# Four quarter-width column tiles for a GLU gate, and w_down's rows in the same order: one decode step on one Trainium2 core

## The chip, the core and the metric

The kernel runs on one core of a Trainium2 chip. The core has a matrix engine (TensorE, PE in the profile), a vector engine (DVE), an activation engine (ACT), GpSimd (POOL) and a sync engine (SP). Here SP and ACT issue all transfers. Sixteen DMA engines carry them from the chip's memory into the SBUF, the on-chip memory of 128 partitions. Matrix products go into PSUM. The metric is the device time of one execution in microseconds; the time before is the median of three runs.

## The reference

A decode step for one token: `x` has 512 values. It is normalized, and goes into an attention over 32 heads with 8192 cached keys and values of 128 elements each, and beside it into a gated unit whose result scales that of the attention.

```python
xn = _layernorm(x, axis=-1)                        # 512 values
# attention: wq [512, 4096], caches [1, 32, 8192, 128], wo [4096, 512]
q = (xn @ wq).reshape(B, Sq, H, Dh).transpose(0, 2, 1, 3)
scores = einsum("bhqd,bhkd->bhqk", q, k_cache) * (Dh ** -0.5)
o = einsum("bhqk,bhkd->bhqd", softmax(scores), v_cache)
s = o.transpose(0, 2, 1, 3).reshape(B, Sq, H * Dh) @ wo
# gated unit: w_gate and w_up [512, 1376], w_down [1376, 512]
h = sigmoid(xn @ w_gate) * (xn @ w_up)
g = silu(h @ w_down)
out = x + s * g
```

All of it is float32. The two caches hold 134 MB each (32 x 8192 x 128 x 4 bytes), wq and wo 8.4 MB each, the three matrices of the gated unit 2.8 MB each.

## The kernel before

The kernel treats two heads as a pair. A pair's keys are 16384 rows of 128 values; each partition takes 128 of them, 64 KB in a row. Three buffers of that size, `slots[0]` to `slots[2]`, hold what is in flight: the keys of pair `i` go to `slots[i % 2]`, all values to `slots[2]`. For each pair DVE multiplies the keys by the query (L276) and sums (L277), PE and ACT turn the scores into powers, and PE multiplies these with the values (L250). The normalized result of a pair is put into `o_all` by two small transfers that ACT issues (`place`, L298), of four rows each.

All large transfers go through SP's queue in the order in which they are written, each behind the waits that free its buffer. `load` (L121) issues one transfer and gives it a semaphore; the transfer is done when the semaphore has gone up by 16.

At the end of the loop the queue holds, in this order: the last pair's values into `slots[0]` (L326), `w_gate` and `w_up` (L330 and L331) into `slots[2]` once the matmuls of the values before are done, `w_down` in two transfers behind them (L332 and L333), and `wo` in six pieces into `slots[1]` (L336 to L338), once DVE is done with the last keys. `wo`'s partition `p` holds rows 32p to 32p + 31; `W_ENDS` cuts these 32 rows into pieces of 14, 10, 4, 2, 1 and 1.

The gate (L341 to L387) comes behind the loop on every engine. PE works with one vector of the normalized `x` as its stationary operand, so a matmul has a single output row; four such rows, at the partitions 0, 32, 64 and 96 of a PSUM bank, are called column tiles here (`NG = 4`, `GP = 32`). With F = 1376 the sizes are `FP = 10`, `FW = 320`, `FL = 96` and `FH = 352`. For each of `w_gate` and `w_up`, and each of the `KT = 4` parts of the contraction, tile `g` multiplies columns 320g to 320g + 319 in one matmul, which covers the first 1280 columns. The 96 columns that remain are done by three of the four tiles in matmuls of 32 columns (the loop over `g1` to `NG`). Tile 0 has nothing there, so DVE first zeroes its 32 places in the bank of the up-projection (L343), and PE waits for that.

ACT takes the sigmoid (L355), DVE multiplies (L358) and turns the row of each tile into columns by ten transposes of 32x32 blocks and one more for the last 32 places (L360 to L362). After that, `hid[p, c]` is hidden value 10p + c. So `w_down` is loaded with rows 10p to 10p + 9 in partition `p` (L332), and its last 128 rows, one in each partition, into `wd_last` (L333). PE multiplies the eleven columns (L377), the four partial rows are copied by ACT and folded by PE (L364 to L374), and ACT and DVE form the silu (L385 and L387).

Then PE goes through `wo` (L390 to L409), piece by piece as the pieces land. DVE multiplies by the gate, adds `x`, and SP stores the output (L411 to L416).

Of the kernel before, what the change touches and what calls it, by code (L numbers as in the profile page):

```python
# [13 lines left out]
P = 128  # L14
# [4 lines left out]
def kernel(  # L19
# [14 lines left out]
    D = x.shape[-1]  # L34
    F = w_gate.shape[1]
    KT = D // P
# [3 lines left out]
    NG = 4  # L40
    GP = P // NG
    GC = D // NG
    QT = 512
    HT = QT // Dh
    NQ = H * Dh // QT
# [3 lines left out]
    SLOT = NB * Dh  # L49
    HALF = (slice(0, HP), slice(HP, P))  # L50

    FP = F // P
    FL = F - FP * P
    FW = FP * GP
    FH = FW + GP
    assert FH <= QT and FL % GP == 0 and 2 * KT * F + FP * D <= SLOT

    W_ENDS, W_FOLD = (14, 24, 28, 30, 31, 32), 28

    PE, DVE, ACT, SP, POOL = nc.tensor, nc.vector, nc.scalar, nc.sync, nc.gpsimd  # L60
# [3 lines left out]
    def sb(name, *shape):  # L64
        return nc.alloc_sbuf_tensor(name, [P, *shape], F32)[:]

    def bank(name, rows, cols):
        return nc.alloc_psum_tensor(name, [rows, cols], F32)[:]


    x_col, xc, sq, xn = (sb(n, KT) for n in ("x_col", "xc", "sq", "xn"))
# [12 lines left out]
    wd_last = q_all[:, :D]  # L84
    sg, hg, s_tmp = (q_all[:, a:a + n] for a, n in ((D, FH), (D + FH, FH), (D + 2 * FH, QT)))
    assert D + 2 * FH + QT <= NP * Dh and FH <= QT

# [3 lines left out]
    o1 = sb("o1", QT)  # L91
    hid = o1[:, :(FP + 1) * GP].rearrange("p (c i) -> p c i", i=GP)

    o_all = sb("o_all", WR)

    big = [bank(f"big{i}", P, QT) for i in range(2)]
# [7 lines left out]
    def semaphore(name):  # L104
        sems.append(nc.alloc_semaphore(name))
        return sems[-1]
# [11 lines left out]
    pe, dve, act, pool = (Steps(n) for n in ("s_pe", "s_dve", "s_act", "s_pool"))  # L118
    loads = {}

    def load(eng, name, dst, src, *after):  # L121
        wait(eng, *after)
        if name not in loads:
            loads[name] = [semaphore(f"s_{name}"), 0]
        loads[name][1] += 16
        eng.dma_start(dst, src).then_inc(loads[name][0], 16)  # L126
        return loads[name][0], loads[name][1]

    def wait(eng, *steps):
        for s in steps:  # L130
            if s is not None:
                eng.wait_ge(*s)
# [42 lines left out]
    t = dve(DVE.reduce_sum(st[:, 0:1], x_col, axis=AX.X))  # L175
    wait(PE, t)
    t = pe(PE.matmul(pt[:, 0:1], ones, st[:, 0:1], start=True, stop=True))
    wait(DVE, t)
    t = dve(DVE.tensor_scalar(st[:, 1:2], pt[:, 0:1], 1.0 / D, None, op0=ALU.mult))
    wait(DVE, t)  # L180
    t = dve(DVE.tensor_scalar(xc, x_col, st[:, 1:2], None, op0=ALU.subtract))
    wait(DVE, t)
    t = dve(DVE.tensor_mul(sq, xc, xc))
    wait(DVE, t)
    t = dve(DVE.reduce_sum(st[:, 2:3], sq, axis=AX.X))
    wait(PE, t)
    t = pe(PE.matmul(pm[:, 0:1], ones, st[:, 2:3], start=True, stop=True))
    wait(ACT, t, c_eps)
    t = act(ACT.activation(st[:, 3:4], pm[:, 0:1], AF.Sqrt, bias=eps_t, scale=1.0 / D))
    wait(DVE, t)  # L190
    t = dve(DVE.reciprocal(st[:, 4:5], st[:, 3:4]))
# [5 lines left out]
    for k in range(KT):  # L197
        for b in range(NQ // NG):
            for g in range(NG):
                c = (b * NG + g) * QT  # L200
                ins = PE.matmul(big[b][g * GP:g * GP + 1, :], xn[:, k:k + 1], wq_t[:, k, c:c + QT],  # L201
                                start=(k == 0), stop=(k == KT - 1))
# [6 lines left out]
    spreads, copies = {}, {}  # L209
    for t in range(NQ):  # L210
        b, g = divmod(t, NG)
        wait(PE, c_row if t == 0 else None, copies.get(t - 2))
        spreads[t] = pe(PE.matmul(big[t % 2], ones[g * GP:g * GP + 1, :], q_row[g * GP:g * GP + 1, b, :],  # L213
                                  start=True, stop=True))

        for u in (t,) if t < NQ - 2 else (NQ - 2, NQ - 1) if t == NQ - 1 else ():
            wait(ACT, spreads[t])
            q = big[u % 2].rearrange("p (i e d) -> p i e d", e=2, d=Dh)
# [108 lines left out]
    t = slots[2]  # L327
    wg_t, wu_t = (t[:, n * KT * F:(n + 1) * KT * F].rearrange("p (k f) -> p k f", f=F) for n in range(2))
    wd_t = t[:, 2 * KT * F:2 * KT * F + FP * D].rearrange("p (c e) -> p c e", e=D)
    ld_g = load(SP, "wg", wg_t, w_gate.rearrange("(p k) f -> p k f", k=KT), (valued, NP - 1))  # L330
    ld_u = load(SP, "wu", wu_t, w_up.rearrange("(p k) f -> p k f", k=KT))  # L331
    load(SP, "wd", wd_t, w_down[:FP * P, :].rearrange("(p r) e -> p r e", r=FP))  # L332
    ld_d = load(SP, "wd", wd_last, w_down[F - P:, :])  # L333
    wo_t = slots[(NP - 1) % 2].rearrange("p (r e) -> p r e", e=D)
    ld_o = []
    for n, (r0, r1) in enumerate(zip((0,) + W_ENDS, W_ENDS)):  # L336
# [1 line left out]
                         summed[NP - 1] if n == 0 else None))  # L338


    g0 = (P - FL) // GP  # L341
    wait(DVE, copies[NQ - 1])
    c_zero = dve(DVE.memset(big[1][:g0 * GP, FW:FH], 0.0))  # L343
    wait(PE, c_zero)
    rows = []
    for dst, src, ld in ((big[0], wg_t, ld_g), (big[1], wu_t, ld_u)):
        wait(PE, ld)
        for c0, f0, w, g1 in ((0, 0, FW, 0), (FW, F - P, GP, g0)):
            for k in range(KT):
                for g in range(g1, NG):  # L350
                    ins = PE.matmul(dst[g * GP:g * GP + 1, c0:c0 + w], xn[:, k:k + 1],
                                    src[:, k, f0 + g * w:f0 + (g + 1) * w], start=(k == 0), stop=(k == KT - 1))
        rows.append(pe(ins))
    wait(ACT, rows[0])
    t = act(ACT.activation(sg, big[0][:, :FH], AF.Sigmoid))  # L355
    wait(DVE, t, rows[1])
    c_p4 = dve(DVE.memset(big[0], 0.0))
    t = dve(DVE.tensor_mul(hg, sg, big[1][:, :FH]))  # L358
    wait(DVE, t)
    for c in range(FP):  # L360
        dve(DVE.transpose(hid[:, c, :], hg[:, c:FW:FP]))
    t = dve(DVE.transpose(hid[:, FP, :], hg[:, FW:]))  # L362

    def to_fold(after):  # L364
        wait(ACT, after)
        return act(ACT.copy(s_tmp, big[0]))
# [10 lines left out]
    for c in range(FP + 1):  # L377
        g = c % NG * GP
        ins = PE.matmul(big[0][g:g + 1, :], hid[:, c, 0:1], wd_t[:, c, :] if c < FP else wd_last,
                        start=(c < NG), stop=(c + NG > FP))  # L380
    t = to_fold(pe(ins))
# [3 lines left out]
    t = act(ACT.activation(g_row, big[1][:, :GC], AF.Sigmoid))  # L385
# [6 lines left out]
    for ld, r1 in zip(ld_o, W_ENDS):  # L392
        wait(PE, ld)
        for r in range(r0, r1):
            if r < W_FOLD:
                g = r % NG * GP
                ins = PE.matmul(big[0][g:g + 1, :], o_all[:, r:r + 1], wo_t[:, r, :],  # L397
                                start=(r < NG), stop=(r + NG >= W_FOLD))
                continue
            for g in range(NG):  # L400
                ins = PE.matmul(acc[g * GP:g * GP + 1, :], o_all[:, r:r + 1], wo_t[:, r, g * GC:(g + 1) * GC],  # L401
                                start=(r == W_FOLD), stop=(r == WR - 1))
# [8 lines left out]
    t = dve(DVE.tensor_mul(g_row, g_row, acc))  # L411
    wait(DVE, t)
    t = dve(DVE.tensor_add(g_row, g_row, x_row))  # L413
# [37 lines left out]
```

## Time and profile before

| what | value |
|---|---|
| median of 3 runs | 687.94 us (687.91 to 688.11) |
| the profiled execution | 687.58 us |
| its span, first to last instruction | 685.8 us |
| mean granted TensorE clock | 0.659 |
| DVE busy | 574.0 us, 84% of the span |
| PE busy | 226.5 us, 33% |
| read from the chip's memory | 293.74 MB, 428 GB/s over the span |

The profile is a page on one execution, and a trace behind it that answers questions. Times in it are microseconds from the start of the span unless marked ns. An engine is busy while an instruction runs on it; "idle before, releaser" names the engine or the transfer that let the next instruction go. The profiled execution took 687.58 us, 1.78 us more than its span, and 0.36 us less than the median of the runs.

### The profile page before, as it was taken

Reading aid. Unit: us, or ns where it says so; the run is one execution under the profiler, and the core shown is the slowest. Engines: PE = TensorE matmul, PEld = TensorE weight load, DVE = VectorE, ACT = ScalarE, POOL = GpSimd, SP = SyncE. Lnnn points to the kernel's source line nnn. Section 1 sums busy time; section 2 is a strip of 40 time slices with the busy share of each in tenths; the row PEclk is TensorE's granted clock in tenths of the full one; section 3 lists DMA queues with packets and bytes.
Section 4 is the critical chain, followed back from the end, with each engine's and each line's share of the span. In section 5 each row is a group of like instructions: output and inputs, shape, how many; then the busy total and the mean of one; then the engine's idle time right before and its main releaser. Section 6 shows DMA issues by size and latency. Waiting matters only on the chain.

```text
span 685.8 us, 3690 instructions
## 1 busy us (share of the span) xinstructions
PE 226.5 (33%) x1570; PEld 63.8 (9%) x1570; DVE 574.0 (84%) x136; ACT 40.9 (6%) x122; POOL 0.7 (0%) x6
## 2 busy tenths in 40 slices
PE   0650230506042240605042150605042150506666
PEld 0110000101000010101000010101001010101121
DVE  1059999999999999989898989989898989989220
ACT  0030100000000000000001010000001010000010
POOL 0000000000000000000000000000000000000000
PEclk9955575756657575757566575757557575756898
DMA  8999999999999999999999999999999999999996
GB/s 371 459 441 436 432 428 428 428 432 428 428 432 466 433 436 428 432 428 432 428 428 428 443 459 432 432 428 432 432 428 428 428 443 451 440 432 428 406 431 283
DMA packets 6614, 293.84 MB, mean 428 GB/s; under 512 B 1096, under 2 KB 1104, under 8 KB 1616
## 3 DMA queue, kind: packets, MB, share of 16 engines
q1 hardware_dynamic: 6200, 293.74, 99.0%
q10 hardware_dynamic: 408, 0.02, 0.0%
q8 instruction: 4, 0.07, 0.0%
q14 instruction: 2, 0.02, 0.0%
HBM read 293.74 MB, written 0.00 MB: 428 GB/s over the span
## 4 chain that ended last, share of the span: by engine, by line
DMA 36%; DVE 30%; SPq 1%; PE 0%; issue 0%
DMA slot<-in_A_k_cache_dram 31%; DVE slot L276 15%; DVE sc L277 15%; DMA slot<-in_A_wo_dram 5%; SPq L126 1%; PE pt L241 0%; PE acc L401 0%; DVE g_row L411 0%; DVE g_row L413 0%; DVE mx L271 0%
## 5 line engine op out<-in xcount | busy, mean ns | idle before, releaser
L276 DVE TENSOR_TENSOR slot<-slot,q_all 128x16384 f32<-128x16384 f32 x16 | 275.5, 17217 | 48.3 <-DMA slot<-in_A_k_cache_dram 48.3
L277 DVE TENSOR_REDUCE sc<-slot 128x128 f32<-128x16384 f32 x16 | 275.5, 17220 | 0.6
L250 PE MATMUL po<-slot,weights 128*8 128x512 f32 x1024 | 148.0, 743 | 231.5 <-PEq L237 230.8
L250 PEld LDWEIGHTS po<-slot,weights 128*8 128x8 f32 x1024 | 30.3, 104 | 336.0 <-issue 335.2
L241 PE MATMUL pt<-ident,mx 128*1 128x128 f32 x32 | 8.7, 372 | 148.6 <-PEq L237 148.6
L296 ACT COPY o<-po 128x512 f32<-128x512 f32 x16 | 9.4, 585 | 385.9 <-PE po L250 385.9
L255 PE MATMUL pn<-o,pick 128*2 128x128 f32 x128 | 16.5, 272 | 12.8 <-PEq L237 12.8
L241 PEld LDWEIGHTS pt<-ident,mx 128*1 128x1 f32 x32 | 1.8, 80 | 154.1 <-issue 154.1
L289 ACT ACTIVATE nb<-pm 128x2 f32<-128x2 f32 x16 | 2.8, 172 | 190.3 <-PE pm L243 190.3
L283 DVE RECIPROCAL rl<-pn 2x1 f32<-2x1 f32 x16 | 2.3, 146 | 13.8 <-PE pn L255 13.8
L291 ACT ACTIVATE weights<-sc,nb 64x128 f32<-64x128 f32 x32 | 12.8, 399 | 0.9
L255 PEld LDWEIGHTS pn<-o,pick 128*2 128x2 f32 x128 | 9.9, 84 | 29.6 <-issue 27.2
L201 PE MATMUL big<-slot,xn 128*1 128x512 f32 x64 | 9.6, 768 | 7.5 <-DMA slot<-in_A_wq_dram 7.5
L411 DVE TENSOR_TENSOR g_row<-g_row,acc 128x128 f32<-128x128 f32 x1 | 0.3, 286 | 13.6 <-PE acc L401 13.6
L243 PE MATMUL pm<-mx,ones 1*128 1x2 f32 x32 | 8.8, 343 | 7.4 <-PEq L237 7.4
L245 PE MATMUL pn<-rs,half 128*2 128x1 f32 x32 | 3.0, 163 | 23.6 <-PEq L237 23.6
L397 PE MATMUL big<-slot,o_all 128*1 128x512 f32 x56 | 9.6, 802 | 2.9 <-DMA slot<-in_A_wo_dram 2.9
L213 PE MATMUL big<-q_all,ones 1*128 1x512 f32 x16 | 9.7, 1011 | 1.7 <-ACT q_all L220 0.8
L175 DVE TENSOR_REDUCE st<-x_col 128x1 f32<-128x4 f32 x1 | 0.2, 157 | 10.9 <-DMA x_col<-in_A_x_dram 10.9
L243 PEld LDWEIGHTS pm<-mx,ones 1*128 1x128 f32 x32 | 7.9, 306 | 14.3 <-issue 14.3
L271 DVE TENSOR_REDUCE mx<-pt 1x2 f32<-1x128 f32 x16 | 4.5, 279 | 5.1 <-PE pt L241 4.8
L220 ACT COPY q_all<-big 64x256 f32<-64x256 f32 x16 | 5.9, 366 | 6.4 <-PE big L213 6.1
(61 smaller groups left out, 60.4 us busy)
## 6 DMA issues: line engine op xcount, KB each, us to landing
slot<-in_A_wo_dram SPq DMA_DIRECT2D x1, 3584.0 KB, 32.6
slot<-in_B_w_gate_dram SPq DMA_DIRECT2D x1, 2752.0 KB, 16.2
slot<-in_B_w_up_dram SPq DMA_DIRECT2D x1, 2752.0 KB, 22.2
slot<-in_B_w_down_dram SPq DMA_DIRECT2D x1, 2560.0 KB, 26.7
slot<-in_A_wo_dram SPq DMA_DIRECT2D x1, 2560.0 KB, 38.3
slot<-in_A_wo_dram SPq DMA_DIRECT2D x1, 1024.0 KB, 40.3
o_all<-on ACTq DMA_DIRECT2D x32, 0.5 KB
slot<-in_A_wo_dram SPq DMA_DIRECT2D x1, 512.0 KB, 41.0
```

The lines of the kernel that those rows point to most:

```text
L126: eng.dma_start(dst, src).then_inc(loads[name][0], 16)
L201: ins = PE.matmul(big[b][g * GP:g * GP + 1, :], xn[:, k:k + 1], wq_t[:, k, c:c + QT], start=(k == 0), stop=(k == KT - 1))
L213: spreads[t] = pe(PE.matmul(big[t % 2], ones[g * GP:g * GP + 1, :], q_row[g * GP:g * GP + 1, b, :], start=True, stop=True))
L241: PE.matmul(pt[0:1, :], mx[:, 0:1], ident, start=True, stop=True).then_inc(turned, 1)
L243: PE.matmul(pm, ones[:1, :], mx[:1, 1:3], start=True, stop=True).then_inc(spread_m, 1)
L250: ins = PE.matmul(po[g * GP:g * GP + 2 * HT, :], weights[:, j // HT, :], v[:, j * Dh:(j + HT) * Dh], start=(j < HT * NG), stop=(j >= NB - ...
L255: ins = PE.matmul(pn[:, :Dh], pick[:, b:2 * HT:HT], o1[:, b * Dh:(b + 1) * Dh], start=(b == 0), stop=(b == HT - 1))
L276: wait(DVE, dve(DVE.tensor_mul(k, k, qb[:, i:i + 1, :].to_broadcast([P, NB, Dh]))))
L277: summed[i] = dve(DVE.reduce_sum(sc[i % 2], k, axis=AX.X))
L291: ACT.activation(weights[h, :, e * HT:(e + 1) * HT], sc[i % 2][h].rearrange("p (g b) -> p g b", b=HT), AF.Exp, bias=nb[h, e:e + 1], scale= ...
L296: ACT.copy(o1, po).then_inc(copied, 1)
L397: ins = PE.matmul(big[0][g:g + 1, :], o_all[:, r:r + 1], wo_t[:, r, :], start=(r < NG), stop=(r + NG >= W_FOLD))
```

## The change

The 1376 columns are cut into four quarters of 344. Each column tile takes its quarter in one matmul for each part of the contraction, so the matmuls of 32 columns, the zeroed places and PE's wait for them are dropped. `FP` stays 10 and `FW` 320, now as 344 // 32 and ten times 32; `FH` is 344.

A tile's hidden values are then 344g to 344g + 343. The ten transposes take the first 320 of each tile, and the eleventh the last 32. These overlap by eight places, which DVE zeroes in `hg` ahead of the eleventh transpose and behind the ten, with a wait on each side. `w_down` is loaded to match: viewed as four blocks of 344 rows, the first transfer takes the first 320 rows of each block, ten to a partition, and the second the last 32 rows of each block, one to a partition.

```diff
-    FP = F // P
-    FL = F - FP * P
+    FH = F // NG
+    FP = FH // GP
     FW = FP * GP
-    FH = FW + GP
-    assert FH <= QT and FL % GP == 0 and 2 * KT * F + FP * D <= SLOT
+    FR = FH - FW
+    assert FH <= QT and FH * NG == F and 2 * KT * F + FP * D <= SLOT
...
-    load(SP, "wd", wd_t, w_down[:FP * P, :].rearrange("(p r) e -> p r e", r=FP))
-    ld_d = load(SP, "wd", wd_last, w_down[F - P:, :])
+    wd = w_down.rearrange("(g f) e -> g f e", g=NG)
+    load(SP, "wd", wd_t, wd[:, :FW, :].rearrange("g (q r) e -> g q r e", r=FP))
+    ld_d = load(SP, "wd", wd_last, wd[:, FH - GP:, :])
...
-    g0 = (P - FL) // GP
-    wait(DVE, copies[NQ - 1])
-    c_zero = dve(DVE.memset(big[1][:g0 * GP, FW:FH], 0.0))
-    wait(PE, c_zero)
+    wait(PE, copies[NQ - 1])
     rows = []
     for dst, src, ld in ((big[0], wg_t, ld_g), (big[1], wu_t, ld_u)):
         wait(PE, ld)
-        for c0, f0, w, g1 in ((0, 0, FW, 0), (FW, F - P, GP, g0)):
-            for k in range(KT):
-                for g in range(g1, NG):
-                    ins = PE.matmul(dst[g * GP:g * GP + 1, c0:c0 + w], xn[:, k:k + 1],
-                                    src[:, k, f0 + g * w:f0 + (g + 1) * w], start=(k == 0), stop=(k == KT - 1))
+        for k in range(KT):
+            for g in range(NG):
+                ins = PE.matmul(dst[g * GP:g * GP + 1, :FH], xn[:, k:k + 1], src[:, k, g * FH:(g + 1) * FH],
+                                start=(k == 0), stop=(k == KT - 1))
         rows.append(pe(ins))
...
     for c in range(FP):
-        dve(DVE.transpose(hid[:, c, :], hg[:, c:FW:FP]))
-    t = dve(DVE.transpose(hid[:, FP, :], hg[:, FW:]))
+        t = dve(DVE.transpose(hid[:, c, :], hg[:, c:FW:FP]))
+
+    wait(DVE, t)
+    wait(DVE, dve(DVE.memset(hg[:, FH - GP:FW], 0.0)))
+    t = dve(DVE.transpose(hid[:, FP, :], hg[:, FH - GP:]))
```

## The prediction

> **What bounds the kernel now.** I read the page first, for the share of the transfers.
>
> ```profile
> span 685.8 us, 3690 instructions
> DMA  8999999999999999999999999999999999999996
> q1 hardware_dynamic: 6200, 293.74, 99.0%
> q10 hardware_dynamic: 408, 0.02, 0.0%
> ```
>
> SP's queue (q1) keeps the sixteen DMA engines occupied for 99.0% of the span; only the last slice drops. Then the table by stages, for two pairs in the middle (its columns end with the granted clock, the DMA share and GB/s):
>
> ```profile
> 177.20:254.50 77.30, 22.59 (x156) 6.37 (x156) 76.42 (x13) 3.48 (x12) 0.00 (x0) 0.63 1.00 433
> ```
>
> A DMA share of 1.00 goes with 433 GB/s, 27.1 GB/s for each of sixteen engines. Third, the chain that ended last, for the end of the kernel:
>
> ```profile
> 638.19 0.33 SPq L126
> ...
> 639.99 4.29 SPq L126
> ...
> 644.32 37.52 DMA slot<-in_A_wo_dram
> ...
> 681.88 0.44 PE acc L401 x8
> ...
> 682.35 0.30 DVE g_row L411
> ...
> 682.67 0.29 DVE g_row L413
> ```
>
> The end hangs on the last piece of wo, which lands at 681.84. Behind it stand only 1.1 us of PE and DVE work. The gate is not in the chain. Its place is seen in the timeline:
>
> ```profile
> 633.51 0.43 SPq L126 DMA_DIRECT2D slot<-in_B_w_up_dram  x1
> 633.99 0.43 SPq L126 DMA_DIRECT2D slot<-in_B_w_down_dram  x1
> 634.46 0.43 SPq L126 DMA_DIRECT2D q_all<-in_B_w_down_dram  x1
> 653.64 0.09 DVE L343 MEMSET big<- 32x32 f32 x1
> 653.78 4.95 PE L351 MATMUL big<-slot,xn 128*1 128x320 f32 x112 [0.71 <-DVE big L343]
> 661.14 0.17 DVE L362 STREAM_TRANSPOSE o<-q_all 128x32 f32<-128x32 f32 x1
> 662.50 3.79 PE L379 MATMUL big<-slot,o 128*1 128x512 f32 x18 [3.76 <-DMA q_all<-in_B_w_down_dram]
> 668.41 0.29 DVE L387 TENSOR_TENSOR g_row<-g_row,big 128x128 f32<-128x128 f32 x1 [0.16 <-ACT g_row L385]
> 670.93 0.14 PEld L397 LDWEIGHTS big<-slot,o_all 128*1 128x1 f32 x8 [3.19 <-issue]
> 670.96 9.56 PE L397 MATMUL big<-slot,o_all 128*1 128x512 f32 x56 [2.92 <-DMA slot<-in_A_wo_dram]
> 676.92 0.10 PEld L397 LDWEIGHTS big<-slot,o_all 128*1 128x1 f32 x6 [0.75 <-DMA slot<-in_A_wo_dram]
> 680.59 0.32 PEld L401 LDWEIGHTS acc<-slot,o_all 128*1 128x1 f32 x16 [1.01 <-DMA slot<-in_A_wo_dram]
> 681.88 0.10 PEld L401 LDWEIGHTS acc<-slot,o_all 128*1 128x1 f32 x8 [0.35 <-DMA slot<-in_A_wo_dram]
> ```
>
> The hidden values are ready at 661.3, but PE waits for w_down until 662.5; the gate is done at 668.7, and PE then waits 2.9 us for the first piece of wo. So the gate's arithmetic has 1.2 us of room and then 2.3 us more, while any delay in the queue of transfers is paid in full.
>
> **The change, part by part.** *Gate matmuls.* L351 has 112 records in 4.95 us: 64 of 320 columns and 48 of 32 (each matmul leaves two). They become 64 of 344. The four tiles run beside each other, so a projection costs about what its wide matmuls cost: that makes 4.95 us into some 4.6. PE also starts up to 0.7 us earlier without L343's zeroing. Both end in the wait for w_down: gain 0. *DVE.* Added are two waits and a zeroing of 128x8. L343's own 0.09 us is the nearest row for the zeroing; with the last transpose no longer overlapping the ten before it (0.17 us), it is 0.3 to 0.5 us, within the 1.2 us of room. What queues behind on DVE (L383) waits for ACT anyway. Cost 0; without that cover it would be 0.5 us at most.
>
> *The two loads of w_down.* Bytes, order and length of a row stay: 128 pieces of 20 KB and 128 of 2 KB. What changes is the shape on the memory's side: 128 equal steps before, four blocks of 32 rows with a gap between them now. Does the spread over the engines depend on that? The rows on transfers tell something:
>
> ```profile
> slot<-in_A_wo_dram SPq DMA_DIRECT2D x1, 3584.0 KB, 32.6
> slot<-in_B_w_gate_dram SPq DMA_DIRECT2D x1, 2752.0 KB, 16.2
> slot<-in_B_w_up_dram SPq DMA_DIRECT2D x1, 2752.0 KB, 22.2
> slot<-in_B_w_down_dram SPq DMA_DIRECT2D x1, 2560.0 KB, 26.7
> slot<-in_A_wo_dram SPq DMA_DIRECT2D x1, 2560.0 KB, 38.3
> ...
> o_all<-on ACTq DMA_DIRECT2D x32, 0.5 KB
> ...
> slot<-in_A_wo_dram SPq DMA_DIRECT2D x2, 256.0 KB, 39.4
> ...
> q_all<-in_B_w_down_dram SPq DMA_DIRECT2D x1, 256.0 KB, 27.9
> x_col<-in_A_x_dram ACTq DMA_DIRECT2D x1, 2.0 KB, 12.5
> ...
> x_row<-in_A_x_dram ACTq DMA_DIRECT2D x1, 2.0 KB
> ```
>
> ACT's queue (q10) has 408 packets for 34 transfers: 32 placings of four rows, x_row with four rows, and x_col with 128. If a transfer leaves one packet for each row and one "done" for each engine that took part, then four engines for four rows give 33 x (4 + 4) and 128 + 16 for x_col: 264 + 144 = 408, exactly. With sixteen engines for all it would be 804, with one for the small ones 309. So the number of engines follows the outermost count. The new loads have 128 on the SBUF's side and 4 on the memory's side. No row has two different counts; if one division must serve both sides, it is four: one engine for each block of 344 rows. I take that.
>
> [...]
>
> The price: each of the four engines takes 32 pieces of each load, where each of sixteen took eight. The nearest row is wo's second piece: 2560 KB, as large as w_down's first load and also with 20 KB in each partition. Its landing is 676.92 - 670.93 = 5.99 us behind the piece before it. Four times as much on an engine takes 23.96, so it adds 17.97 us. For the 256 KB load the nearest rows are wo's last two pieces of that size: from 680.59 to 681.88, 0.645 us each, so it adds 3 x 0.645 = 1.94. Sum: 19.9 us. A faster pace for the four while the rest are idle I leave out: 27.1 GB/s is what an engine shows at a share of 1.00. The other end of the price is the second rival below.
>
> All of this is on the path. wo is queued behind w_down on the same engines, and a piece of wo counts as landed only when all sixteen parts are in, the four late ones among them. The other twelve finish early and gain nothing. PE gets w_down at 662.4 + 19.9 = 682.3, and needs 6.2 us from there to the end of the gate (662.5 to 668.7): 688.5. The first wo piece comes at 670.9 + 19.9 = 690.8, so the gate stays off the path, and the tail of 1.1 us is the same. SP itself: its fifth wo issue stands 4.29 us until the last values have landed, so there is a limit on what is outstanding. With fuller queues on four engines SP will stand longer, and the twelve may run dry. That costs nothing as long as the four have work, and SP stands only when they have much.
>
> Sum for the profiled execution: 687.58 (span 685.8 and 1.78 around it) + 19.9 = 707.5. The median lies 0.36 above that execution: **707.8 us**.
>
> **The rivals.** *Second: four engines, in each other's way.* The 27.1 GB/s may belong to the engine, or to the entrance to the partitions that it fills; before, each engine has eight partitions of its own, and the rows can't tell these apart. In the new load the four engines walk through four blocks of 32 partitions, all at the same row of their block at about the same time. If two such rows share an entrance, each of the four gets half the pace: 64 x (5.99 / 8) = 47.9 us, and 8 x 0.645 = 5.2, less the 6.6 of before: +46.4, or 734.3. If two engines are a few pieces apart, so that they meet half of the time, it is one and a half times the price instead of twice: 39.8 - 6.6 = +33.2, or 721.1. If the wo pieces of the other twelve also push through the same entrances for their first 14.4 us (8.4 for 3584 KB and 6.0 for 2560 KB at the pace above), a third of the pace is left instead of a half, and 4.8 us more are lost: 739.1. It decides as soon as two engines are less than a few rows apart. For it speaks that one ceiling holds everywhere; against it, that no row shows a transfer below 27.1 GB/s an engine.
>
> [...]
>
> *Third, the other side: sixteen engines after all.* If the SBUF's 128 partitions set the spread, or the load goes out as four transfers of 32 partitions on sixteen engines, the queue is as long as before. The gate's 0.3 us and 0.7 us then vanish in the wait for w_down, and the time is 687.9, not slower. For it: every load of 128 partitions so far shows the full rate. Against it: none of them has a gap between blocks. It decides wherever the emitted outermost count on both sides is a multiple of sixteen.
>
> *Fourth:* something longer, for instance one engine for a load (15 times the 6.6 us, +100 us), or SP's limit leaving even the four without work.
>
> **How the numbers follow.** Four engines at full pace 0.44; four in each other's way 0.36; sixteen engines 0.15; longer 0.05. The forecast is the first, 707.8. Its own range is 704 to 712. The lower end takes another row for the price: w_up lands at 633.51 + 22.2 = 655.7 and w_down's first load at 633.99 + 26.7 = 660.7, only 5.0 us behind it, which makes 15.0 + 1.9 = 16.9 us, or 704.8. The upper end allows for a tenth of the second case. The range that is asked reaches over the second, from 704 to 741, and leaves out 0.20. Between 712 and 721 lies the case in which the four meet only now and then. A difference of 0.2% (1.4 us) is about what a measurement of this kernel can tell from no change. Slower by more: 0.85, the first, second and fourth. Within it: 0.13. Faster: 0.02, if the freed PE time let something go earlier that the trace doesn't show.
>
> **What would show it.** On four engines q1 would have 24 packets fewer, 6176, for twice twelve missing "done" packets. From about 662 on, the DMA share would fall to a quarter for some time, at 108 GB/s by the first case and 54 by the second. w_down's first load would take 26.7 + 18.0 = 44.7 us from issue to landing, by the second case 62 to 69. PE's wait for w_down before L379's successor would grow from 3.8 to about 24 us by the first, 50 by the second, and PE would wait again, for about 2 us, before the first wo piece. L351's successor should have 64 records. With 6200 packets and 26.7 us the forecast would be wrong at its root; with 6176 packets and a share below a quarter for longer than 20 us, in its price. If the gate's end came behind the first wo piece, the cover that I counted on would be gone.

## The result, and the profile after

The changed kernel takes 739.61 us (median of five runs, 738.21 to 739.81); the kernel before, beside it, 687.91 us (687.61 to 688.11). The ratio is 1.0745, with a 95% interval of 1.0731 to 1.0760: 51.7 us slower. The prediction was 707.8 with a range of 704 to 741, so the sign and the range held and the forecast itself fell 32 us short.

The page of the changed kernel, its lines on the span and on the transfers:

```profile
span 737.8 us, 3594 instructions
DMA  9999999999999999999999999999999999999631
...
q1 hardware_dynamic: 6176, 293.74, 95.2%
q10 hardware_dynamic: 408, 0.02, 0.0%
```

The bytes are the same 293.74 MB. There are 24 packets fewer on q1, just the two times twelve missing "done" packets of a load on four engines. The last slices are now six, three and one tenths busy instead of nine, nine and six.

The timeline of the changed kernel, at the gate and behind it (start, duration, engine, line; L349 is the old L351, L380 the old L379, L388 the old L387, L398 the old L397, L402 the old L401):

```profile
638.59 69.02 SPq L127 DMA_DIRECT2D slot<-in_A_wo_dram  x6
...
652.77 2.48 PE L349 MATMUL big<-slot,xn 128*1 128x344 f32 x29
...
656.68 2.49 PE L349 MATMUL big<-slot,xn 128*1 128x344 f32 x32 [1.43 <-DMA slot<-in_B_w_up_dram]
...
660.38 1.27 DVE L359 STREAM_TRANSPOSE o<-q_all 128x32 f32<-128x32 f32 x10
661.72 0.07 DVE L362 MEMSET q_all<- 128x8 f32 x1
661.82 0.21 DVE L363 STREAM_TRANSPOSE o<-q_all 128x32 f32<-128x32 f32 x1
714.55 4.43 PE L380 MATMUL big<-slot,o 128*1 128x512 f32 x18 [55.38 <-DMA q_all<-in_B_w_down_dram]
...
721.31 0.29 DVE L388 TENSOR_TENSOR g_row<-g_row,big 128x128 f32<-128x128 f32 x1 [0.16 <-ACT g_row L386]
...
722.99 5.30 PE L398 MATMUL big<-slot,o_all 128*1 128x512 f32 x28 [2.06 <-DMA slot<-in_A_wo_dram]
...
733.92 0.10 PEld L402 LDWEIGHTS acc<-slot,o_all 128*1 128x1 f32 x8 [0.36 <-DMA slot<-in_A_wo_dram]
```

Up to the second projection little has moved: w_up is there at 656.7, 1 us later than before (633.51 + 22.2 = 655.7). Then PE waits 55.4 us for w_down, where it waited 3.8. From w_down's arrival to that of the first wo piece it is 8.4 us (714.55 to 722.99), as before (8.5), and the rest of the kernel follows at its old distances. So nearly all of the loss lies between 656.7 and 714.5: 57.9 us from w_up to w_down, where it was 6.8 (655.7 to 662.5).

The table by stages of the changed kernel, for three stretches (the last three columns are the clock, the DMA share and GB/s):

```profile
658.00:690.00 32.00, 1.17 (x19) 0.21 (x8) 2.44 (x14) 0.00 (x0) 0.00 (x0) 0.57 0.99 189
698.00:704.00 6.00, 0.00 (x0) 0.00 (x0) 0.00 (x0) 0.00 (x0) 0.00 (x0) 0.50 0.24 66
716.00:720.00 4.00, 3.83 (x18) 0.42 (x10) 0.00 (x0) 0.11 (x1) 0.00 (x0) 0.50 0.25 106
```

Three states can be read here. From 658 to 690 all sixteen engines count as busy (0.99) and together move 189 GB/s, less than half of the 433 that the same share gave before. From 698 to 704 only four are busy, at 66 GB/s. From 716 on, when w_down is in and the four work off their part of wo, four move 106 GB/s. So an engine that counts as busy can run at its full pace (106 over four is 26.5 GB/s), at 16 GB/s (66 over four), or at 12 (189 over sixteen). The forecast's own sum had only the first.

### The profile page after: what moved, and what is told of

It reads as the page before. It is cut to its first block, busy times and chain, and to the rows that moved or that the text cites. A ratio compares the mean times of both kernels' runs of the same rounds, so it can differ in the third digit from the quotient of the medians.

```text
span 737.8 us, 3594 instructions
## 1 busy us (share of the span) xinstructions
PE 226.5 (31%) x1522; PEld 62.9 (9%) x1522; DVE 574.1 (78%) x136; ACT 40.9 (6%) x122; POOL 0.7 (0%) x6
## 3 DMA queue, kind: packets, MB, share of 16 engines
q1 hardware_dynamic: 6176, 293.74, 95.2%
HBM read 293.74 MB, written 0.00 MB: 398 GB/s over the span
## 4 chain that ended last, share of the span: by engine, by line
DMA 32%; DVE 28%; SPq 9%; issue 0%; PE 0%
DMA slot<-in_A_k_cache_dram 29%; DVE slot L277 14%; DVE sc L278 14%; SPq L127 9%; DMA slot<-in_A_wo_dram 4%; PE pt L242 0%; PE acc L402 0%; DVE on L285 0%; DVE g_row L412 0%; DVE g_row L414 0%; DVE rl L284 0%; DVE mx L280 0%; DVE mx L272 0%
## 5 line engine op out<-in xcount | busy, mean ns | idle before, releaser
L380 PE MATMUL big<-slot,o 128*1 128x512 f32 x20 | 5.3, 1048 | 55.4 <-DMA q_all<-in_B_w_down_dram 55.4
L398 PE MATMUL big<-slot,o_all 128*1 128x512 f32 x56 | 8.9, 722 | 2.7 <-DMA slot<-in_A_wo_dram 2.7
```

## The experiments

**The gate without its loads, and the loads cut in four.** The first kernel keeps the new gate and takes back the shape of the loads; the second keeps the rows and cuts each load by blocks. From here on two readings of the 27.1 GB/s of an engine before the change, both from the prediction's second rival, are set against each other: "engine", by which this is the pace of an engine wherever it writes, and "entrance", by which it is that of the entrance to the partitions that it fills, so that engines which meet at one entrance share its pace. No trace names an entrance; the runs show paces.

```diff
-    wd = w_down.rearrange("(g f) e -> g f e", g=NG)
-    load(SP, "wd", wd_t, wd[:, :FW, :].rearrange("g (q r) e -> g q r e", r=FP))
-    ld_d = load(SP, "wd", wd_last, wd[:, FH - GP:, :])
+    load(SP, "wd", wd_t, w_down[:FP * P, :].rearrange("(p r) e -> p r e", r=FP))
+    ld_d = load(SP, "wd", wd_last, w_down[F - P:, :])
```

> The changed gate as it is, but w_down loaded in the old shape: 128 equal steps of ten rows on the memory's side, and the last 128 rows. So PE multiplies with other rows of w_down than the hidden values belong to; bytes and rows per partition are the same. All theories put the loss on the loads, and the gate's arithmetic behind the transfers: time within 0.2% of before, 687.9 us, w_down landed at about 662.5 and q1 with 6200 packets. A rest of the loss here would mean that the new waits of DVE and PE are not hidden.

Measured: 687.71 us against 687.83, ratio 1.0001 (0.9992 to 1.0010). In its timeline the hidden values are ready 1.4 us before w_down:

```profile
661.31 0.21 DVE L362 STREAM_TRANSPOSE o<-q_all 128x32 f32<-128x32 f32 x1
662.93 4.43 PE L379 MATMUL big<-slot,o 128*1 128x512 f32 x18 [4.27 <-DMA q_all<-in_B_w_down_dram]
```

Its queue q1 has 6200 packets again. The new matmuls, DVE's waits and the zeroing cost nothing, and they gain nothing. All 51.7 us belong to the two loads.

```diff
-    load(SP, "wd", wd_t, wd[:, :FW, :].rearrange("g (q r) e -> g q r e", r=FP))
-    ld_d = load(SP, "wd", wd_last, wd[:, FH - GP:, :])
+    for g in range(NG):
+        load(SP, "wd", wd_t[g * GP:(g + 1) * GP], wd[g, :FW, :].rearrange("(q r) e -> q r e", r=FP))
+    for g in range(NG):
+        ld_d = load(SP, "wd", wd_last[g * GP:(g + 1) * GP], wd[g, FH - GP:, :])
```

> The changed kernel with each load of w_down cut into four, one for each block of 344 rows, each into 32 partitions: 32 equal steps on both sides, so sixteen engines with two rows each, done 16 times for each of eight transfers. Theory 'engine' (27.1 GB/s is the ceiling of an engine, wherever it writes): 6.6 us for w_down as before, 687.9 us in all. [...]

Measured: 696.41 us against 687.83, ratio 1.0123 (1.0108 to 1.0139), 8.6 us slower than before. The table by stages, for the load and for wo behind it, and the arrivals of w_up and w_down at PE:

```profile
656.00:672.00 16.00, 2.85 (x37) 0.73 (x32) 2.44 (x14) 1.61 (x2) 0.00 (x0) 0.77 0.96 206
672.00:688.00 16.00, 11.68 (x66) 2.03 (x70) 0.77 (x2) 0.86 (x2) 0.00 (x0) 0.70 0.98 416
...
659.13 2.50 PE L351 MATMUL big<-slot,xn 128*1 128x344 f32 x32 [2.77 <-DMA slot<-in_B_w_up_dram]
...
672.98 4.43 PE L382 MATMUL big<-slot,o 128*1 128x512 f32 x18 [11.35 <-DMA q_all<-in_B_w_down_dram]
```

Sixteen engines are busy in both (q1 has 6296 packets, 96 more than before, as sixteen "done" packets for each of six more transfers make), yet into 32 partitions at a time they move half of what they move into 128, 206 GB/s against 416. "Engine" falls here: the pace also depends on where the engines write. From w_up to w_down it is 13.9 us (659.1 to 673.0), twice the 6.8 of before (655.7 to 662.5), and so what half the pace makes; but w_up itself came 2.4 us later than in the changed kernel (656.7), so the first blocks of w_down seem to have slowed its rest already. The execution that is profiled here is the slowest of four, at 697.91 us.

**The four engines alone.** In the next four kernels SP waits for w_down before it issues wo, so nobody works beside the load. These kernels, and the three behind them, were timed once each.

```diff
+    wait(SP, ld_d)
     ld_o = []
```

> The changed kernel, with SP waiting until w_down has landed before it issues any piece of wo, so that the four engines are alone from about 657 on. 'Engine' (the long time came from the crowd: wo's pieces beside w_down, and SP's long stand): w_down takes 26.5 us, lands at about 683, then wo needs 2 + 19.4 and the tail: span about 709. 'Entrance' (two of the four meet all the way): 53 us, landed at about 710, span about 735; if they are a few rows apart, 40 us and 722.

> As held4, but w_down goes out in eight transfers of 16 partitions and eight more for the last rows. Each has four steps with a gap on the memory's side, so it still has four engines, with four rows each; but these fill neighbouring groups of four partitions, not blocks that are 32 apart. The same bytes of w_down are read; they come into other partitions, so the product is not w_down's. 'Entrance': nobody meets, w_down takes 26.5 us, landed at about 684, span about 709. 'Engine': the same. If it is as slow as held4, the shape of the transfer or the mere number of four engines costs, and 'entrance' falls.

The second of these loads in transfers of 16 partitions:

```diff
-    load(SP, "wd", wd_t, wd[:, :FW, :].rearrange("g (q r) e -> g q r e", r=FP))
-    ld_d = load(SP, "wd", wd_last, wd[:, FH - GP:, :])
+    for n in range(8):
+        load(SP, "wd", wd_t[16 * n:16 * n + 16], wd[:, 4 * FP * n:4 * FP * (n + 1), :].rearrange("g (q r) e -> g q r e", r=FP))
+    for n in range(8):
+        ld_d = load(SP, "wd", wd_last[16 * n:16 * n + 16], wd[:, FH - GP + 4 * n:FH - GP + 4 * n + 4, :])
```

Measured: the first has a span of 723.7 (725.54 us), the second of 709.6 (711.57 us), the 709 that was expected. From the first, the stage of the load and PE's wait:

```profile
658.00:690.00 32.00, 0.20 (x4) 0.00 (x0) 2.44 (x14) 0.00 (x0) 0.00 (x0) 0.54 0.25 71
...
696.50 4.43 PE L381 MATMUL big<-slot,o 128*1 128x512 f32 x18 [38.30 <-DMA q_all<-in_B_w_down_dram]
```

And from the second:

```profile
658.00:680.00 22.00, 0.27 (x4) 0.00 (x0) 2.44 (x14) 0.00 (x0) 0.00 (x0) 0.57 0.25 106
...
682.18 3.66 PE L383 MATMUL big<-slot,o 128*1 128x512 f32 x18 [23.91 <-DMA q_all<-in_B_w_down_dram]
```

In both, four engines are busy and nobody else (share 0.25). With blocks 32 partitions apart they move 71 GB/s, with neighbouring groups of four 106 GB/s. Between w_up and w_down lie 40.8 us in the first (655.7 to 696.5) and 26.6 in the second (655.6 to 682.2). The 26.5 us of the forecast was thus right for four engines in neighbouring groups. The 71 is more than the 54 that "entrance" gives for a meeting all the way: by that reading they meet for part of the time, not always. The trace has the time of every single packet too, and there it can be seen: while the load is alone, each row of 20 KB takes 0.76 us in the second kernel, as it did before the change, and from 0.76 to 1.60 us in the first. By the edits, with one engine to a block as the author took it, each of the four has the same block of rows to read in both kernels, in the same order, so the memory's side is not the cause. Nor is the number of transfers: sixteen small ones lose nothing here (106 GB/s).

Then the number of engines was varied, with `g=8` and `g=2` blocks in place of four, so with blocks of 16 and of 64 partitions:

```diff
-    wd = w_down.rearrange("(g f) e -> g f e", g=NG)
-    load(SP, "wd", wd_t, wd[:, :FW, :].rearrange("g (q r) e -> g q r e", r=FP))
-    ld_d = load(SP, "wd", wd_last, wd[:, FH - GP:, :])
+    wd = w_down.rearrange("(g f) e -> g f e", g=8)
+    load(SP, "wd", wd_t, wd[:, :FP * P // 8, :].rearrange("g (q r) e -> g q r e", r=FP))
+    ld_d = load(SP, "wd", wd_last, wd[:, F // 8 - P // 8:, :])
```

> As held4, with wo held back, but w_down cut into eight blocks (172 rows apart), so eight engines with blocks of 16 partitions. Other rows of w_down are read than the hidden values belong to; bytes are the same. 'Engine': twice the pace of four engines on groups of their own, 217 GB/s, 13.3 us, landed at about 669. 'Entrance': blocks 16 apart, so engines 0 and 2 meet, 1 and 3, and so on: 109 GB/s if in step, 125 to 155 if they drift as in held4; landed at 676 to 683.

> As held4, but two blocks (688 rows apart), so two engines, each with 64 partitions that never share an entrance with the other's. Other rows of w_down are read. Both theories: 54 GB/s, 53 us, landed at about 709. The point is the comparison: by 'entrance' two engines are nearly as fast as four in blocks 32 apart (62 to 77 GB/s there), by 'engine' they would have half their pace.

Eight engines, the stage and the queue's row:

```profile
660.00:680.00 20.00, 1.31 (x20) 0.28 (x12) 2.44 (x14) 0.00 (x0) 0.00 (x0) 0.59 0.48 107
...
q1 hardware_dynamic: 6184, 293.74, 96.8%
```

Two engines:

```profile
658.00:706.00 48.00, 0.74 (x9) 0.08 (x1) 2.44 (x14) 0.00 (x0) 0.00 (x0) 0.54 0.13 54
...
q1 hardware_dynamic: 6172, 293.74, 92.4%
```

The packets again count the engines: 16 fewer for twice eight missing, 28 fewer for twice fourteen. Eight engines move 107 GB/s, as much as four in neighbouring groups (106); two move 54, each at its full 27. "Entrance" gave 109 for eight that meet in step, "engine" 217; both gave 54 for two. Which engines meet, the trace does not name. That blocks 32 partitions apart do, as the first of these expectations takes it, is a reading of the 71 GB/s of four engines there, where neighbouring groups have 106; two in blocks 64 apart lose nothing (54). The spans are 709.3 (711.09 us) and 736.2 (737.98 us).

**The crowd.** Alone, blocks 32 apart cost 40.8 us; in the changed kernel, with wo beside them, 57.9 (656.68 to 714.55). And the twelve engines that carry only wo there were busy until about 692 (the DMA share is 0.94 in the 4 us before it and 0.42 in the 4 us behind it). The first test puts wo beside the four engines in neighbouring groups, which is the kernel of sixteen small transfers without SP's wait:

> As held4_own (four engines, neighbouring groups of partitions, sixteen small transfers), but wo is issued at once, as in the changed kernel, so the other twelve engines fill partitions beside the four. This asks what the crowd costs: alone the four took 26.5 us here, and 41 us in blocks 32 apart, where the crowd made it 58. Theory 'shared entrances only': an engine is slowed only where it meets another; the four meet a third party for part of the time, w_down lands at 685 to 695, and the span is 707 to 715. Theory 'a clogged entrance slows everybody': all sixteen drop to about 215 GB/s together as in the changed kernel, w_down lands after 700, and the span is above 720.

```profile
664.00:692.00 28.00, 0.00 (x0) 0.00 (x0) 0.00 (x0) 0.00 (x0) 0.00 (x0) 0.50 0.99 211
...
699.19 4.43 PE L382 MATMUL big<-slot,o 128*1 128x512 f32 x18 [41.05 <-DMA q_all<-in_B_w_down_dram]
```

Measured: 211 GB/s for sixteen busy engines, w_down at 699.2 instead of 682.2, span 722.3 (724.07 us). That speaks for the clog, but also for any two transfers side by side. The next two kernels separate these. Both load w_down in the old shape, and add 2 MB on four engines; only the partitions that these fill differ. That the four meet nobody in the first and four of the other twelve in the second was the author's assumption, since the trace does not name an engine's partitions. (At the very end SP waits for these loads too.)

```diff
+    vx = rows_of(v_cache, 0).rearrange("(g q) x -> g q x", g=NG)
+    for n, p0 in enumerate((0, 32)):
+        ld_x = load(SP, "extra", slots[NP % 2][p0:p0 + 16], vx[:, 4 * n:4 * n + 4, :], (valued, NP))
     wo_t = slots[(NP - 1) % 2].rearrange("p (r e) -> p r e", e=D)
```

> w_down in the old shape on sixteen engines (so with other rows than the hidden values belong to), and between w_down and wo 2 MB more that nobody uses: rows of 64 KB from the value cache into the free buffer slots[0], on four engines, into partitions 0 to 15 and then 32 to 47. [...] Each of the four has 512 KB more: 19.4 us. Both theories of the crowd: about 430 GB/s while all sixteen work, span 705 to 707. If all fall to about 215 here too, two transfers side by side are enough, and neither shared entrances nor a clog is the cause.

> As extra_own, but the 2 MB go into partitions 64 to 79 and 96 to 111, the groups of four of the other twelve engines, while these fill them with wo. 'Shared entrances only': eight engines at half their pace and eight at full, about 325 GB/s while all work, the four need about 30 us instead of 19.4 and the span is 710 to 718. 'A clogged entrance slows everybody': about 215 GB/s for all sixteen, and the span is 716 to 726.

The stage in which wo runs beside the 2 MB, first with partitions 0 to 15 and 32 to 47, then with 64 to 79 and 96 to 111:

```profile
664.00:680.00 16.00, 3.73 (x26) 0.58 (x18) 0.77 (x2) 0.86 (x2) 0.00 (x0) 0.61 0.98 417
```

```profile
664.00:696.00 32.00, 5.13 (x30) 0.68 (x22) 0.77 (x2) 0.86 (x2) 0.00 (x0) 0.55 0.99 201
```

The first has a span of 705.3 (707.05 us). That is 18.9 us above the kernel before that was timed beside it (688.15), about the 19.4 that 2 MB on four engines were to cost, and there are 417 GB/s in the crowd. The second has 725.5 (727.28 us): same source, same bytes, four engines again (6240 packets in both), 20 us more, and 201 GB/s. Of the twelve engines with wo, only four would fill partitions that the extra load touches, if each has eight partitions of its own; that is an estimate, from the eight rows of 28 KB at 1.06 us that make the 8.5 us of wo's first piece before the change. Had the other eight gone on at 27 GB/s, they would have been done with wo in some 19 us and the share would have fallen to a half; it stayed at 0.99 for 32 us. The single packets show it directly: of the rows of wo's first piece (28 KB) that begin in these windows, every one takes 1.06 us in the first kernel, as before the change, and 2.24 us or more in the second. So with nothing changed but the partitions of the extra load, all sixteen fall to about half (201 GB/s against 417). SP's long stand is not the cause: in the second kernel it had issued all of wo by 656.6.

```profile
653.73 2.87 SPq L127 DMA_DIRECT2D slot<-in_A_wo_dram  x6
```

## Why the prediction was wrong

**What bounds the kernel: right.** The queue of transfers is the bound, and the gate's arithmetic stands behind it: with the old loads the new gate takes 687.71 us against 687.83. The cover that was named was there in the changed kernel too: the gate ends at 721.6, and PE waits 2.06 us for the first piece of wo.

**The gate's own terms: one of two mis-sized, without effect.** The eleventh transpose ends 0.38 us behind the tenth (660.38 + 1.27 to 662.03), within the 0.3 to 0.5 that was given. The matmuls did not become cheaper: 2.49 us for a projection, so 4.98 for both, where 4.6 was expected and 4.95 stood before. The tiles did run beside each other in the trace of before, as was taken: L351's 64 wide records have 0.43 us each, and all 112 stand in 4.95 us. The narrow matmuls that were dropped had cost nearly nothing beyond what the wider ones now take.

**Four engines: right.** The step from the packet counts of transfers of four rows to "one division must serve both sides" held for the case that no row had shown: 6176 packets with four blocks, 6184 with eight, 6172 with two. The third rival, sixteen engines after all, is out.

**The price: wrong, and this is the step that failed.** "Each of the four engines takes 32 pieces", at the 5.99 us for eight that wo's second piece had shown, made 26.5 us for w_down. It took 57.9. That row was measured with sixteen engines on 128 partitions; in the runs above the pace depends on the partitions too, with four engines at 71 GB/s in blocks 32 apart and at 106 in neighbouring groups. The runs split the missing 31 us:

| between w_up's and w_down's arrival at PE | us |
|---|---|
| four engines in neighbouring groups, wo held back | 26.6 |
| four engines in blocks 32 apart, wo held back | 40.8 |
| the changed kernel, wo beside them | 57.9 |

So some 14 us come with the blocks 32 apart, and 17 with the crowd. The crowd costs as much where the four fill neighbouring groups: w_down came at 682.2 with wo held back and at 699.2 beside it.

**The other twelve: half right.** They were to "finish early and gain nothing". They did end before the four, at about 692, and gained nothing, but they were slowed as well: from 656 to 672 a row of wo's first piece took at least 1.67 us, against 1.06 before. SP's stand grew from 12 us for the six issues to 69. That it would grow was said, and it did not let the four run dry: from 716 to 720 they still move 106 GB/s. The forecast took the stand of the fifth issue before the change to last until the last values had landed; it ended at 644.28, 2 us after these values had released PE (642.30), so what it waited for is open.

**The second rival: right in kind, and its number partly by luck.** It gave 721.1 for meeting half of the time, 734.3 for meeting always, and 739.1 with wo pushing through the same entrances; 739.6 was measured. But the four lost less than a meeting all the way makes (40.8 us for w_down alone, not 53.1), and the crowd costs 17 us rather than the 4.8 of that sum, with all sixteen slowed (189 GB/s). The two misses, 12 us each, cancel. No run shows the shared entrance that this rival's sums are made from. What the runs show in its place are paces: with wo held back 54 GB/s for two engines in blocks of 64 partitions, 107 for eight in blocks of 16, 71 for four in blocks of 32 and 106 for four on neighbouring groups, and with wo queued behind 206 for sixteen engines on 32 partitions. A sharing of the pace agrees with these. For the crowd it is not enough, since all sixteen were slowed (201 GB/s against 417). The rival was given 0.36 because no row of before bore on it.

Left open is by which path a load on four engines slows all sixteen: the runs show, for loads from the chip's memory, that it does (201 GB/s instead of 417), but not where a path is shared. It also stays open why all of them settle near half of their pace (2.24 us or more for a row of 28 KB, against 1.06).

No version here is clearly faster than the kernel before. With the gate's arithmetic behind the transfers, little can be expected in this part except from fewer bytes or an emptier queue; that was not tried. Of the versions with the new row order, four loads of 32 partitions are the best at 696.4; even the mere wait of SP, which leaves twelve engines idle for 40 us, gains 14 us over the changed kernel (725.5).

## What to carry to other kernels

Before a load is reshaped, look at the outermost count on both sides of it: in these runs two, four and eight blocks with gaps on the memory's side meant two, four and eight engines (6172, 6176 and 6184 packets), although the other side had 128 partitions. Then ask which partitions are filled at the same moment; the pace of a row in the profile held only for the pattern in which it was measured (27.1 GB/s for an engine before, 16 and 12 in the changed kernel). A transfer on a few engines can be worth keeping away from others in the queue: here the mere wait was worth 14 us (725.5 against 739.6). And a busy DMA share says nothing of the pace: 0.99 or 1.00 went with anything from 189 to 433 GB/s.

## What the runs showed of the hardware that was not expected

- Two loads side by side lost no pace with the smaller one in partitions 0 to 15 and 32 to 47 (417 GB/s), and all sixteen engines fell to half with it in 64 to 79 and 96 to 111 (201 GB/s with the same source and bytes).
- Eight engines in blocks of 16 partitions were as fast (107 GB/s) as four on neighbouring groups of four (106), and two engines in blocks of 64 (54) reached three quarters of four in blocks of 32 (71).
- Holding back a queue that had work was the faster way: 725.5 us with SP waiting, 739.6 without.
